# Order of loads on one DMA queue: column reloads behind the next weight chunks, and token tiles 14 and 15 loaded five stages later

## The chip, the cores and the metric

One core of a Trainium2 chip runs the whole kernel. The metric is the device time of one execution in microseconds (us). The time before is the median of three runs.

The core has a matrix engine (PE in the profile, with its weight loads as PEld), a vector engine (DVE), a scalar engine (ACT), a general engine (POOL) and a sync engine (SP). SP computes nothing: it issues transfers between the off-chip memory (HBM) and the on-chip memory in the order of the program. Sixteen DMA engines carry them out.

## The reference, cut to what matters

```python
x  = A_x                                   # 1 x 2048 x 512
xn = layernorm(x)
q, k, v = split(xn @ wqkv)                 # 32 heads of 16
pq, pk  = phi(q), phi(k)                   # phi(t) = (t+1 if t>0 else exp(t)) + 1e-6
kv = einsum("bhsd,bhse->bhde", pk, v);  z = sum_s pk
attn = (pq @ kv) / (pq . z + 1e-6) @ wo
h   = relu(xn @ w1 + b1) ** 2              # 512 -> 1376
out = x + attn + h @ w2 + b2
```

## The kernel before, in words

The 2048 tokens are cut into 16 tiles of 128 (NT = 16). Four tiles make a block (TB = 4), so there are four blocks. Numbers are float32, and most operands of products are held as a high and a low part, so that a product is three passes of the matrix engine over 128x512 operands.

**Stage 1, keys of every tile (loop over `i` at L801).** A tile is loaded by `load_x` (L157, transfer at L159), its mean and variance are measured on DVE (`measure`, L230), it is normalised into `xp`, and it must be transposed to become "columns" (features on the partitions). From tile 4 on this goes through HBM: `regroup` (L277) stores normalised tiles to a scratch tensor `via` (L281) and appends four reads to a list; `move` (L286) issues the listed reads at L289, into `xg` (into `xg4s` for tiles 4 and 5); DVE turns blocks of 32x32 (`turn`, L293) into a tile `t`, or `xT` for tiles 8 and up; ACT makes the high part `xs0h`/`xs1h` (L324) and DVE the low part `xs0l`/`xs1l` (L327). Then PE projects the columns of tile i onto the key weights (`project`, L369, 12 products into `pk`) and adds the outer products of the tile before it (`kx`, L389, 12 products). Tiles 4 and 5 are stored to `via` one by one, later tiles in pairs.

There are only two sets of columns, `xsb` (`xs0h`, `xs0l` and `xs1h`, `xs1l`), one block of four tiles each. So the columns of blocks 0 and 1 are stored to HBM, `xsd`, when blocks 2 and 3 are about to overwrite them: two stores of 1 MB at i = 4 and two at i = 7 (L811).

Raw tiles `x` alternate between two buffers of two tiles each (`two`, L91) beside two larger ones, so tiles 14 and 15 go where tiles 2 and 3 were.

**Stage 2, queries and the two-layer part, two passes (`for n in range(2)`, L941).** Pass 0 handles blocks 3 and 2, pass 1 blocks 1 and 0 (`t1`, `t2`). At the end of pass 0 a loop over `e` (L1285) adds the products of the second layer for one hidden chunk per step (`mlp_2`, 12 products on PE), while DVE, ACT and SP prepare pass 1. In that loop, in the order of the program:

```python
1289  if e:
1290      do(w2next, 2)                  # split the next piece of w2: high on ACT, low on DVE (L122)
...
1294  if e == 2:
1295      load_res(t2)                   # two 512 KB loads of x for the residual
...
1300  if n == 0 and 1 <= e < 5:          # reload of columns, 1 MB each
1302      nc.sync.dma_start(f32((x1, x2)[k][u]), xsd[(t1, t2)[k] - 2][u])
1303  do(prepare, ...)                   # sums of columns for pass 1, DVE and ACT (L671, L122)
1305  if e == 4:                         # last, narrow chunk of w1
1306      z = pair("w1z1"); zs = small_chunk(z)
1308  if e == 5: w = load_1("q", 0)      # two chunks of query weights, "rq"
1310  if e == 7: zs()                    # split of that chunk of w1, ACT then DVE (L119)
```

`small_chunk` loads by `raw_1` (three transfers at L184, named `r`, in runs of 256 and 128 bytes); the query weights are loaded at L714. These weights and the pieces of w2 (`r`, L165 and L207) rotate through six raw buffers, so each load waits for the last reader of the load six places before it. The narrow chunk of w1 takes the buffer of piece 4 of w2; the two query chunks take those of pieces 3 and 2. A wait on SP holds every transfer behind it. A transfer's semaphore, one of eight in turn, must also have been met by the transfer eight places before.

After the loop come the attention products of the four tiles (`add_attention`), the last two hidden chunks (`wait_for(last_two[...])`, which makes `s` from `r2c` on ACT and DVE, and for the narrow chunk copies a part of `s` by a transfer at L468), the sums to the output (L1054, stores at L1058), and pass 1 begins with `plain_1`, which reads the reloaded columns `xs0h`, `xs0l` and the narrow chunk; the columns `xs1h`, `xs1l` are first read a few products later. POOL adds the second bias to the residual by transfers of its own (L1046).

Of the kernel before, what the change touches and what calls it, by code (L numbers as in the profile page):

```python
# [18 lines left out]
def kernel(  # L19
# [58 lines left out]
    def bank(name, tag="ps"):  # L78
        return psum.tile([P, 512], F32, name=name, tag=tag)
# [6 lines left out]
    def next_tag(of):  # L86
        k, n = turns[of]
        turns[of][0] = (k + 1) % n
        return f"{of}{k}"

    def two(name):  # L91
        return keep.tile([P, 2, 512], F32, name=name, tag=next_tag("x"))
# [7 lines left out]
    def f32(ap):  # L100
        return ap.bitcast(F32)
# [55 lines left out]
    def load_x(i, t):  # L157
        n = t.shape[1]
        nc.sync.dma_start(t, xf[i * P:(i + n) * P, :].rearrange("(i p) d -> p i d", i=n))  # L159
        for k in range(n):  # L160
            xr[i + k] = t[:, k]
# [11 lines left out]
    def units(f):  # L173


        if f < NF - 1:
            return [(0, f * P, P)]
        return [(0, f * P + Q, 2 * Q), (2 * Q, f * P, Q), (3 * Q, f * P, Q)]

    def raw_1(f):  # L180
        t = w512(f"r1_{f}", "raw", 6)
        tj = t.rearrange("p (j n) -> p j n", j=NJ)
        for a, o, n in units(f):
            nc.sync.dma_start(tj[:, :, a:a + n], w1[:, o:o + n].rearrange("(j p) n -> p j n", j=NJ))  # L184
        return t
# [3 lines left out]
    def load_o():  # L189
        o = wos[0] = four("wo", "ra")  # L190
        for j in range(NJ):
            cut = P - Q * j
            for a, z, to in ((0, cut, Q * j), (cut, P, 0)):
                if z > a:
                    nc.sync.dma_start(o[to:to + z - a, j], wo[j * P + a:j * P + z, :])
# [52 lines left out]
    def normalise(tiles, st, mv, y):  # L248

        n = len(tiles)  # L250
        r, u = (y[:, k, :n] for k in range(2))
        if tiles[-1] >= NPE:

            nc.vector.scalar_tensor_tensor(u, mv[:, :n, 0], -1.0, r, op0=OP.mult, op1=OP.mult)
        later = []

        def last(i, o, src, k):
            nc.scalar.activation(o, src, AF.Identity, bias=u[:, k:k + 1], scale=r[:, k:k + 1])
            if i in groups:
                regroup(i)  # L260

        for k, i in enumerate(tiles):
            o, src = xp[i], xr[i]
            if i >= NDVE:

                o, src = o.rearrange("p g (j c) -> p g j c", j=NJ), gjc(src)
            if i < NPE:
                nc.vector.tensor_scalar(o, src, mv[:, k, 0:1], r[:, k:k + 1], op0=OP.subtract, op1=OP.mult)
                if i in groups:
                    regroup(i)  # L270
            else:
                later.append(lambda a=(i, o, src, k): last(*a))
        return later
# [12 lines left out]
    def move(n=8):  # L286
        for _ in range(n):
            if moves:
                nc.sync.dma_start(*moves.pop(0))  # L289
# [9 lines left out]
    def cols(i):  # L299

        return xsb[(i // TB + 1) % 2]
# [64 lines left out]
    def project(i, ps, w, steps, first=True, last=True):  # L366

        for n, (j, u, v) in enumerate(steps):
            nc.tensor.matmul(ps, lhsT=cols(i)[u][:, j, slot(i)], rhs=w[v][:, j, :], start=first and n == 0,  # L369
                             stop=last and n == len(steps) - 1)  # L370

    def parts(i):

        p = kp[i]
        pk[i] = pair(f"pk{i}")
        copy("act", pk[i][:, 0], p, 1e-6)
        nc.vector.scalar_tensor_tensor(pk[i][:, 1], p, 1e-6, f32(pk[i][:, 0]), op0=OP.add, op1=OP.subtract)
# [168 lines left out]
    for i0 in range(0, NT, TB):  # L546
# [5 lines left out]
        n = TB if i0 >= NPE else TB // 2  # L552
        if i0 < NPE:
            single = work.tile([P, 2, 512], F32, name=f"xg{i0}s", tag="r0")
            for k in range(2):
                i = i0 + k
# [3 lines left out]
        for k in range(0, n, 2):  # L560
            i = i0 + TB - n + k
            u, v = (t.rearrange("p a (g c) -> p (a g c)", g=NJ) for t in (a[:, TB - n + k:][:, :2], o[:, k:k + 2]))
            groups[i + 1] = [t.rearrange("p (g n) -> p g n", g=NJ) for t in (u, v)]
            u, v = (t.rearrange("p (g i c) -> p g i c", g=NJ, i=2) for t in (u, v))
# [89 lines left out]
    parts(0)  # L654
    phi_k(1, pks[1])
    normalise(*single)
    load_x(14, two("x14"))
    parts(1)
    tokens(1, "dve")
    measure(soon)  # L660
# [4 lines left out]
    def tokens_sum(n, tag):  # L665
        return keep.tile([P, 2, 2, 512], F32R, name=f"T{n}", tag=tag)
# [32 lines left out]
    def fetch():  # L699
        while todo and len(held) < 3:  # L700
            held.append(todo.pop(0)())
# [89 lines left out]
    def more(i=None):  # L791

        if i is None or i > 12:
            do(extra, counts[0].pop(0))
# [6 lines left out]
    for i in range(2, NT):  # L801
        if i == 13:
            nc.sync.dma_start(b1s[:, :NF - 1], b1[:(NF - 1) * P].rearrange("(f p) -> p f", p=P))
            for a, o, n in units(NF - 1):
                nc.sync.dma_start(b1s[a:a + n, NF - 1:], b1[o:o + n, None])
        move()
        if i in (4, 7):

            b = i // 7
            for u in range(2):  # L810
                nc.sync.dma_start(xsd[b][u], f32(cols(b * TB)[u]))  # L811
        if i == 9:
            load_o()
        if i > 10:
            fetch()
        ps = pks[i] if i < 3 else bank(f"pk{i}")
        if i > 2:
            project(i, ps, wk, HL)
        high = low = keep_t = lambda: None
        if i < NDVE:  # L820
            high, low, keep_t = transposed(i + 1)
        later = normalise(*soon) if i == 3 else []

        soon_turned = transposed(i + 2) if 11 <= i and i + 2 < NT else ()

        def mid():
            high()
            more(i)

        def late():  # L830
            low()
            more(i)

        if i == 12:
            rawz = raw_1(NF - 1)
            T.update({n: tokens_sum(n, f"B{n - 1}") for n in (1, 2)})
        if i == 12:
            w = load_1("q", 0)
        if i == 13:
            todo_1 = operands_first(0, w)  # L840
            extra.append(todo_1.pop(1))
        if i == 14:
            z = pair("w1z0")
            extra.append(lambda: split(z[:, 0], z[:, 1], rawz, "act", "dve"))
            o34 = halves(four("Tf", "r0"))
            extra.extend(sums_of(xT[NB - 1], xT[NB - 2], *o34))
            lows = [extra.pop() for k in range(2)]
            extra += [todo_1[0], lows[1], todo_1[1], lows[0], *todo_1[2:]]
        phi_k(i, ps, mid, late)
        more(i)  # L850
        run(*soon_turned)
        if i != 3:
            later = normalise(*soon) if soon else []
        parts(i)
        keep_t()
        if i == 2:
            tokens(2)
        if i + 1 < NT:
            tokens(i + 1)
        run(*later)  # L860
        if NDVE < i + 2 < 13:
            run(*transposed(i + 2))
        pieces(int(i > 11))
        if i == 2:
            ahead[3] = statistics(6, 7)
        if i + 2 in (4, 6, 8, 10):
            ahead[i + 2] = group(i + 6, i + 7)
        if i < 10:
            measure(ahead[(i + 2) // 2 * 2], i % 2)
        soon = ahead.get(i + 1, ())  # L870
        if soon:
            roots(*soon)
        kx(i - 1)
        more(i)
# [66 lines left out]
    for n in range(2):  # L941
# [128 lines left out]
        for p in range(NO + 1):  # L1070
            at_p = AT[p]
            kind, k = order[p] if p < NO else ("", 0)
            fa, fb = 2 * k, 2 * k + 1

            was, k = order[p - 1] if p else ("", 0)
# [209 lines left out]
        for e, f in enumerate(waiting[:-2]):  # L1285
            mlp_2(acc, f, s.pop(f))
            if e + 3 < NF - 2:
                wait_for(waiting[e + 3])
            if e:
                do(w2next, 2)  # L1290
                if e + 8 < NF:
                    g = waiting[e + 8]
                    w2next.extend(piece_2(g, place(g)))
            if e == 2:
                load_res(t2)
            if e == 4:
                bias = add_bias()
            if e in ((5, 6) if n else (7, 8)):
                do(bias)
            if n == 0 and 1 <= e < 5:  # L1300
                k, u = divmod(e - 1, 2)
                nc.sync.dma_start(f32((x1, x2)[k][u]), xsd[(t1, t2)[k] - 2][u])
            do(prepare, (1, 0, 0, 1, 0, 2, 2, 3, 1, 3, 1)[e])
            if n == 0:
                if e == 4:
                    z = pair("w1z1")
                    zs = small_chunk(z)
                if e == 5:
                    w = load_1("q", 0)
                if e == 7:  # L1310
                    zs()
            step(AE[e])
            if e and 0 < len(parts_2) and len(steps[t2]) <= 5 * (len(parts_2) - 1):
                do(parts_2)
# [55 lines left out]
```

## Time and profile before

| what | us |
|---|---|
| median of three runs | 410.63 |
| lowest and highest of them | 410.39, 410.93 |
| the profiled execution, its own time | 410.41 |
| its span, first to last instruction | 408.7 |
| PE busy | 403.8 |
| DVE busy | 304.7 |
| ACT busy | 262.2 |

The mean granted clock of PE was 0.999. The span is the part that the profile shows; 1.7 us of the profiled execution's time lie around it. In the rows below, the first number is a start in microseconds after the span's beginning and the second a duration; a name such as `xs1h<-xT` says which tile is written from which; `x4` counts merged instructions; a bracket at a row's end gives idle time of the engine just before and what ended it. SPq marks issues on the SP queue, whose duration is that of the issuing only. In rows on transfers the last number is the time from issue to landing. An end of a product on PE is modelled by the profiler, its start is not.

### The profile page before, as it was taken

The page shows a single profiled execution, that of the slowest core. Times are in us where ns is not written, and L with a number is a line of the kernel's source. Part 1 is how long each engine was busy: PE and PEld are TensorE (multiplying, and loading weights), DVE is VectorE, ACT ScalarE, POOL GpSimd, SP SyncE. Part 2 cuts the span into 40 slices and gives each one's busy share as a digit, 9 for nine tenths or more (in the row PEclk, how much of TensorE's full clock was granted, in tenths as well). Part 3 has the DMA queues.
Part 4 walks back from the last instruction along what each step waited for, and adds up shares of the span by engine and source line. Part 5 has one row for each costly group of instructions (what it writes and reads, how often), then busy time and mean ns, then how long its engine had stood idle before and what let it go on. Part 6 is the DMA issues. An engine that isn't in the chain of part 4 may idle for free.

```text
span 408.7 us, 5630 instructions
## 1 busy us (share of the span) xinstructions
PE 403.8 (99%) x1943; PEld 331.7 (81%) x1943; DVE 304.7 (75%) x556; ACT 262.2 (64%) x459; POOL 48.5 (12%) x81
## 2 busy tenths in 40 slices
PE   8999999999999999999999999999999999999996
PEld 7878888888788888888878887888888888878885
DVE  6886667487898989988349956567989586449833
ACT  4656777556888788886818641677587857837520
POOL 6343333220000000030000300000000200001200
PEclk9999999999999999999999999999999999999999
DMA  6969576810432231381557983321121881024612
GB/s 213 332 210 329 204 309 206 254 31 0 119 91 79 77 103 28 109 204 22 215 204 271 326 194 106 113 53 51 51 79 36 229 189 36 2 103 154 105 26 103
DMA packets 47182, 56.87 MB, mean 139 GB/s; under 512 B 8305, under 2 KB 30577, under 8 KB 45874
## 3 DMA queue, kind: packets, MB, share of 16 engines
q1 hardware_dynamic: 44850, 52.32, 39.3%
q0 software_dynamic: 2304, 4.20, 6.3%
q8 instruction: 15, 0.25, 0.2%
q14 instruction: 13, 0.11, 0.1%
HBM read 41.69 MB, written 13.63 MB: 135 GB/s over the span
## 4 chain that ended last, share of the span: by engine, by line
PE 85%; DMA 6%; DVE 5%; issue 1%; SPq 1%; ACT 1%; POOL 1%; DVEq 0%; ACTq 0%
PE b L488 33%; PE acc L130 29%; PE pk L369 9%; PE kx L389 9%; DMA r<-in_B_w_dram 4%; PE acc L499 2%; PE pz L130 1%; DVE s L119 1%; SPq L289 1%; PE b L130 1%; PE pz0b L130 1%; DMA x<-in_A_x_dram 1%; DMA via<-xp 1%; DMA xg4s<-via 1%; PE pt L308 0%
## 5 line engine op out<-in xcount | busy, mean ns | idle before, releaser
L130 PE MATMUL acc<-w2r,s 128*128 128x512 f32 x477 | 113.1, 390 | 0.4 <-DVE s L119 0.4
L130 PEld LDWEIGHTS acc<-w2r,s 128*128 128x128 f32 x477 | 89.4, 188 | 20.1 <-DVE s L119 0.8
L488 PE MATMUL b<-T,aop 128*128 128x512 f32 x336 | 83.4, 389 | 0.0
L488 PEld LDWEIGHTS b<-T,aop 128*128 128x128 f32 x336 | 63.0, 188 | 13.9 <-ACT t L111 0.8
L1046 POOL DMA_DIRECT2D res<-in_B_b_dram x16 | 14.4, 1091 | 277.2 <-DVE dt L430 87.4
L389 PE MATMUL kx<-pk,tok 128*128 128x512 f32 x192 | 46.3, 390 | 0.0
L389 PEld LDWEIGHTS kx<-pk,tok 128*128 128x128 f32 x192 | 35.9, 188 | 7.6
L488 PE MATMUL b<-xs0h,aop 128*128 128x512 f32 x112 | 36.9, 390 | 0.0
L130 PE MATMUL acc<-mh,aTsr 128*128 128x512 f32 x112 | 35.6, 389 | 0.0
L1054 DVE TENSOR_TENSOR res<-acc,res 128x512 f32<-128x512 f32 x16 | 11.0, 692 | 21.5 <-PE acc L130 19.2
L488 PEld LDWEIGHTS b<-xs0h,aop 128*128 128x128 f32 x112 | 21.0, 188 | 4.4
L130 PEld LDWEIGHTS acc<-mh,aTsr 128*128 128x128 f32 x112 | 21.0, 188 | 4.4
L119 POOL TENSOR_TENSOR tok<-xp,tok 128x512 fp32r<-128x512 f32 x15 | 19.8, 1322 | 38.9 <-ACT tok L111 38.9
L122 DVE TENSOR_TENSOR w2r<-r,w2r 128x512 fp32r<-128x512 f32 (+2 forms) x35 | 23.8, 681 | 0.5 <-ACT w2r L111 0.4
L111 ACT ACTIVATE aop<-S 128x512 fp32r<-128x512 f32 x28 | 17.5, 624 | 9.8 <-DVE S L728 9.8
L119 DVE TENSOR_TENSOR aop<-S,aop 128x512 fp32r<-128x512 f32 x28 | 19.3, 688 | 4.8 <-ACT aop L111 4.4
L119 DVE TENSOR_TENSOR s<-c,s 128x512 fp32r<-128x512 f32 x20 | 13.5, 689 | 11.4 <-ACT s L111 11.3
L488 PE MATMUL b<-xs0l,aop 128*128 128x512 f32 x56 | 21.8, 389 | 0.0
L130 PE MATMUL acc<-ml,aTsr 128*128 128x512 f32 x56 | 21.8, 389 | 0.0
L111 ACT ACTIVATE w2r<-r 128x512 fp32r<-128x512 f32 x32 | 19.6, 620 | 3.0 <-DMA out_dram<-res 2.0
L111 ACT ACTIVATE T<-Tf 128x512 fp32r<-128x512 f32 x16 | 9.5, 624 | 16.1 <-DVE Tf L671 16.0
L488 PE MATMUL b<-xs1h,aop 128*128 128x512 f32 x56 | 19.5, 389 | 0.0
(190 smaller groups left out, 742.9 us busy)
## 6 DMA issues: line engine op xcount, KB each, us to landing
r<-in_B_w_dram SPq DMA_DIRECT2D x49, 256.0 KB, 3.0
res<-in_A_x_dram SPq DMA_DIRECT2D x8, 512.0 KB, 4.2
res<-in_B_b_dram POOLq DMA_DIRECT2D x16, 256.0 KB, 5.8
out_dram<-res SPq DMA_DIRECT2D x15, 256.0 KB, 2.1
via<-xp SPq DMA_DIRECT2D x5, 512.0 KB, 3.2
xg<-via SPq DMA_DIRECT2D x20, 128.0 KB, 2.8
xTd<-t SPq DMA_DIRECT2D x8, 256.0 KB, 3.2
x<-in_A_x_dram SPq DMA_DIRECT2D x4, 512.0 KB, 6.4
```

Of the source, the lines that this page charges most:

```text
L111: nc.scalar.activation(o, i, AF.Copy, bias=bias)
L119: ENG[el].tensor_tensor(out=l, in0=src, in1=f32(h), op=OP.subtract)
L122: nc.vector.tensor_tensor(out=l, in0=src, in1=f32(h), op=OP.subtract)
L130: nc.tensor.matmul(ps, lhsT=a[u], rhs=b[v], start=first and n == 0, stop=last and n == 2)
L289: nc.sync.dma_start(*moves.pop(0))
L369: nc.tensor.matmul(ps, lhsT=cols(i)[u][:, j, slot(i)], rhs=w[v][:, j, :], start=first and n == 0, stop=last and n == len(steps) - 1)
L389: nc.tensor.matmul(kxp[c], lhsT=tok[i][:, u, c * P:(c + 1) * P], rhs=pk[i][:, v], start=i == 0 and (u, v) == first, stop=i == NT - 1 and ( ...
L488: nc.tensor.matmul(ps, lhsT=a[u][:, j * P:(j + 1) * P], rhs=b[v][:, j, :], start=first and j == 0 and n == 0, stop=last and j == 1 and n == 2,
L499: nc.tensor.matmul(ps, lhsT=s[u][:, k * P:(k + 1) * P], rhs=w2s[NF - 1][u][:, a:z], start=first and u == 0, stop=stop and u == 1)
L1046: nc.gpsimd.dma_start(r[:, i], b2[None, :].partition_broadcast(P), accum_op=OP.add)
L1054: nc.vector.tensor_tensor(out=r[:, a:z], in0=ps, in1=r[:, a:z], op=OP.add)
```

## The change

Two moves on the SP queue; PE, DVE, ACT and POOL keep their instructions and their order.

- The load of tiles 14 and 15 (512 KB) leaves the place behind the store of tile 4 to `via`. It now stands at i = 4, behind the reads of tiles 6 and 7 from `via` and ahead of the two 1 MB stores of columns to `xsd`.
- At the end of pass 0 the narrow chunk of w1 (three transfers) and the two chunks of query weights are issued one step earlier, and three of the four column reloads later: `xs0h` stays at e = 1, `xs0l`, `xs1h` and `xs1l` go from e = 2, 3, 4 to e = 5, 6, 7. The queue's order is now: `xs0h`, piece 10 of w2, the two residual loads, the narrow chunk, the two query chunks, `xs0l`, `xs1h`, the copy of a part of piece 10 (L211), `xs1l`.

```diff
@@ -654,7 +654,6 @@
     normalise(*single)
-    load_x(14, two("x14"))
     parts(1)
@@ -804,6 +803,8 @@
         move()
+        if i == 4:
+            load_x(14, two("x14"))
         if i in (4, 7):
@@ -1297,15 +1298,15 @@
-            if n == 0 and 1 <= e < 5:
-                k, u = divmod(e - 1, 2)
+            if n == 0 and e in (1, 5, 6, 7):
+                k, u = divmod((1, 5, 6, 7).index(e), 2)
                 nc.sync.dma_start(f32((x1, x2)[k][u]), xsd[(t1, t2)[k] - 2][u])
             do(prepare, (1, 0, 0, 1, 0, 2, 2, 3, 1, 3, 1)[e])
             if n == 0:
-                if e == 4:
+                if e == 3:
                     z = pair("w1z1")
                     zs = small_chunk(z)
-                if e == 5:
+                if e == 4:
                     w = load_1("q", 0)
```

## The prediction

> **What bounds the kernel now.** I read the page first: who is busy, and for how much of the span.
>
> ```profile
> span 408.7 us, 5630 instructions
> PE 403.8 (99%) x1943; PEld 331.7 (81%) x1943; DVE 304.7 (75%) x556; ACT 262.2 (64%) x459; POOL 48.5 (12%) x81
> ```
>
> PE is busy for 99%, and its instructions stay the same. A move of transfers can therefore only win the few places where PE stands still for an operand, and lose where it makes new ones. The second view is PE's waits, the third PE's timeline around them.
>
> ```profile
> PE acc L130 <- DVE s L119: 0.4, 1, 0.4
> ...
> PEld pk L369 <- ACT xs0h L324: 0.5, 1, 0.5
> ```
>
> ```profile
> 26.53 1.29 PE L389 MATMUL kx<-pk,tok 128*128 128x512 f32 x5
> 27.89 0.50 PE L369 MATMUL pk<-wkh,xs0h 128*128 128x512 f32 x1
> ...
> 33.63 2.72 PE pk L369 x12
> ...
> 49.84 0.39 PE L369 MATMUL pk<-wkh,xs1h 128*128 128x512 f32 x1
> ...
> 247.18 0.62 PE L130 MATMUL acc<-w2r,s 128*128 128x512 f32 x2
> 248.21 0.50 PE L130 MATMUL acc<-w2r,s 128*128 128x512 f32 x1 [0.41 <-DVE s L119]
> ```
>
> Twelve products take 2.72, so one starts every 0.227. The brackets use modelled ends, so I count by starts.
>
> - At 248: the two products from 247.18 start at 247.18 and 247.41, so the next was due at 247.64. It starts at 248.21, 0.57 late. It also lasts 0.50 instead of the 0.39 of an undisturbed one, 0.11 more. Price of the stop: 0.57 + 0.11 = **0.68**.
> - At 28: the fifth product from 26.53 starts at 27.44, so the next was due at 27.66 and starts at 27.89. Price: 0.23 + 0.11 = **0.34**.
>
> At 49.84 nothing is late today. That place matters below.
>
> **Part 1, the weights ahead of the reloads.** The chain of waits shows where the stop at 248 comes from; then the SP queue's issues, with two landings.
>
> ```profile
> 224.46 16.91 DMA r<-in_B_w_dram
> ...
> 241.48 0.64 ACT w1z L111
> ...
> 247.55 0.61 DVE s L119
> ```
>
> ```profile
> 221.77 0.47 SPq L1302 DMA_DIRECT2D xs0l<-xsd1l  x1
> ...
> 222.76 0.43 SPq L1302 DMA_DIRECT2D xs1l<-xsd0l  x1
> 223.29 10.97 SPq L184 DMA_DIRECT2D r<-in_B_w_dram  x3
> 234.37 4.51 SPq L714 DMA_DIRECT2D rq<-in_A_wqkv_dram  x2
> ```
>
> ```profile
> xs1l<-xsd0l SPq DMA_DIRECT2D x1, 1024.0 KB, 14.6
> ...
> s<-s SPq DMA_DIRECT2D x1, 128.0 KB, 2.2
> ```
>
> The narrow chunk of w1 is issued behind three reloads of 1 MB and lands at 224.46 + 16.91 = 241.37, behind the last of them (222.76 + 14.6 = 237.4). ACT splits it at once, and DVE's timeline shows what that held up.
>
> ```profile
> 223.99 0.68 DVE L122 TENSOR_TENSOR w2r<-r,w2r 128x512 fp32r<-128x512 f32 x1
> ...
> 228.35 0.69 DVE L122 TENSOR_TENSOR w2r<-r,w2r 128x512 fp32r<-128x512 f32 x1
> ...
> 236.25 1.42 DVE L671 TENSOR_TENSOR Tf<-xT,Tf 128x512 f32<-128x512 f32 x2
> 242.14 0.69 DVE L119 TENSOR_TENSOR w1z<-r,w1z 128x512 fp32r<-128x512 f32 x1 [4.47 <-ACT w1z L111]
> ```
>
> DVE is idle for 4.47 in front of that split, and `s`, for which PE waits at 248, stands further back in DVE's order. With the chunk issued where the reloads were, only the two residual loads are ahead of it. It should land some 10 us before 237.67, when DVE comes to it (236.25 + 1.42). Of the 4.47 there then remains about the ACT split of 0.64, so DVE runs 3.8 earlier and `s` is ready 3.8 - 0.57 = 3.2 before PE asks. The stop goes entirely: **-0.68**. Next in line is nothing of DVE's.
>
> What it costs: the second query chunk needs the buffer of piece 2 of w2, which DVE reads until 228.35 + 0.69 = 229.04 (the first query chunk, until 224.67). SP waits there, and behind it stand the three reloads, the copies at L211 and L468, and then the stores of results. The reloads so start at 229.0 instead of 221.8, 7.3 later, and the last would land near 237.4 + 7.3 = 244.7. The readers:
>
> ```profile
> 252.60 2.72 PE pz L130 x12
> ...
> 259.40 2.72 PE b L130 x12
> ```
>
> The first reads `xs0`, the second `xs1`; with the stop gone both come 0.68 sooner, which leaves about 14 us for the last reload. The cost here is nothing, covered by those products. The tightest is the copy at L468, which the narrow chunk's sums at about 248 need: it would have to be behind 244.7 by 3 us, and alone it takes 2.2.
>
> **Part 2, tiles 14 and 15 later.** Rows of the start on the SP queue, DVE, ACT, and the length of the moved load:
>
> ```profile
> 18.89 0.43 SPq L159 DMA_DIRECT2D x<-in_A_x_dram  x1
> ...
> 20.92 3.66 SPq L289 DMA_DIRECT2D xg4s<-via  x4
> ...
> 34.30 0.43 SPq L811 DMA_DIRECT2D xsd0h<-xs1h  x1
> ...
> 36.99 0.32 SPq L281 DMA_DIRECT2D via<-xp  x1
> ...
> 43.06 1.75 SPq L289 DMA_DIRECT2D xg<-via  x4
> ```
>
> ```profile
> 26.46 0.71 DVE L293 STREAM_TRANSPOSE t<-xg4s 128x512 f32<-128x512 f32 x1 [0.15 <-DMA xg4s<-via]
> ...
> 30.88 0.71 DVE L293 STREAM_TRANSPOSE t<-xg4s 128x512 f32<-128x512 f32 x1 [0.16 <-issue]
> ...
> 47.30 0.71 DVE L293 STREAM_TRANSPOSE xT<-xg 128x512 f32<-128x512 f32 x1 [0.37 <-DMA xg<-via]
> ```
>
> ```profile
> 27.21 0.63 ACT L324 ACTIVATE xs0h<-t 128x512 fp32r<-128x512 f32 x1 [1.47 <-DVE t L293]
> ...
> 48.05 0.63 ACT L324 ACTIVATE xs1h<-xT 128x512 fp32r<-128x512 f32 x1
> ```
>
> ```profile
> x<-in_A_x_dram SPq DMA_DIRECT2D x1, 512.0 KB, 6.0
> ...
> DMA packets 6807, 7.95 MB, mean 248 GB/s; under 512 B 482, under 2 KB 5602, under 8 KB 6547
> ...
> 36.00:43.00 7.00, 7.00 (x32) 5.78 (x31) 4.08 (x7) 4.10 (x8) 1.99 (x3) 1.00 0.99 396
> ```
>
> *The gain.* Tile 4's turn on DVE starts at 26.46, held 0.15 by the reads that follow the 512 KB load. Without the load they land earlier, and ACT (idle for 1.47) and PE follow: **-0.15**. Below: 0, since the next such turn shows the same 0.16 with nothing to wait for. Above: the whole 0.34. I take 0.15, the row of the wait itself.
>
> *The loss.* At i = 4 the load stands ahead of 2 MB of stores and of the store of tiles 8 and 9 to `via`, issued at 36.99, which must land before their reads can be issued at 43.06. From 36 to 43 the DMA engines are 99% busy at 396 GB/s, so what is put in front shifts the rest: 0.524 MB / 396 GB/s = 1.32. (The Trainium skill, "DMA: Bandwidth & Descriptors", section "Anatomy of one DMA — SWDGE (gpsimd) path", has a slope of 436 GB/s for another path, an estimate of 1.20; the sum below would be 0.12 lower by it. The measured rate decides.) DVE turns tile 8 at 47.30 after a wait of 0.37 for those reads, so it takes the shift in full. `xs1h` is ready at 48.05 + 0.63 = 48.68; ACT to PE takes 0.05 (27.21 + 0.63 = 27.84 against 27.89), so PE could start at 48.73 and does at 49.84. The slack is 1.11. The 0.15 of the start comes to DMA and PE alike. The stop is 1.32 - 1.11 + 0.11 = **+0.32**. Below: 0, when the shift is 1.1 or less. Above: 0.524 MB at the mean of 248 GB/s of the stretch from 18 to 50 is 2.11, a stop of 1.11. I take 396, the rate of the stretch itself. By tile 9 DVE should have made it up: no further stop.
>
> **Sum.** -0.68 - 0.15 + 0.32 = -0.51. The profiled execution took 410.41 (span 408.7 and 1.7 around it), which would become 409.9. It lies 0.22 below the median of 410.63, so for the median I forecast **410.1**. A difference of 0.2%, 0.82 here, is about what a measurement can tell from no change, so this is within it.
>
> **Rivals.**
>
> - *Tile 8 is not late.* The load is a read among stores; should they overlap, or should the turn of tile 5 and with it the queue come earlier, the 1.1 of slack holds. Then -0.68 - 0.15 to -0.68 - 0.34: 409.6 to 409.8, faster. Against it speaks the 99%, for it that only 0.2 is missing.
> - *Tile 8 is late by much more: slower.* The moved load took 6.0 to land where a copy with little ahead takes 2.2; if it holds the store of tiles 8 and 9 for those 3.8, PE stops for 3.8 - 1.11 + 0.11 = 2.8 and the sum is +2.0: 412.6. It decides from a shift of 1.8 on (a loss at all), beyond 0.2% from 2.7 on. Against it: the 396 GB/s.
> - *The copy at L468 lands late: slower.* Were nothing moved during SP's wait for the query chunk, the whole lot would land 7.3 later than the narrow chunk did, at 241.37 + 7.3 = 248.7, and the copy 2.2 after it, at 250.9. PE needs it just after 247.64, so it would stop for 3.3 + 0.11, and the sum is -0.68 + 3.41 + 0.17 = +2.9, 413.5. It decides from 3 us behind 244.7 on. Against it: until 229 the residual loads, the biases and the chunk keep the DMA engines at work. (The Trainium skill, same page, "Queues, rings and completion order", speaks for it: a transfer's semaphore lands only after all earlier writes of its DMA engine, so a small copy cannot overtake a reload. No run here shows it yet.)
> - *It does not do what it says at 248.* If another late operand stands behind `s`, part 1 brings nothing: -0.15 + 0.32 = +0.17, 410.8.
>
> **How the numbers follow.** Forecast 0.57, tile 8 not late 0.26, much later 0.08, the copy 0.04, no gain 0.05. Faster by over 0.2% is the first rival, 0.26; slower the second and third, 0.12; the rest 0.62. Low end: 409.6 and 0.1 for the runs' spread, 409.5. High end: the stop of 1.11 with no gain at the start, -0.68 + 1.11 = +0.43, 411.1. The slower rivals lie outside.
>
> **What would show it.** Right: no wait of PE for `s` near 247; the narrow chunk landed before 230; DVE's 4.47 under 1; the first product of tile 4 some 0.15 sooner; a new wait of PE for `xs1h` at 49.7, 0.2 to 0.4 long, behind reads issued 1.3 later. Wrong: no such wait, or one over 1; a wait near 247 for the copy or near 252 or 259 for columns.

## The result, and the profile after

| | before | after |
|---|---|---|
| median, us | 410.73 (6 runs, 410.07 to 411.07) | 415.08 (6 runs, 413.83 to 417.94) |
| ratio after to before | | 1.012 (1.0083 to 1.0157) |
| profiled execution, its span | 410.41, 408.7 | 417.94, 416.2 |

The changed kernel is slower by 1.2%, 4.4 us, where 0.5 us less was forecast in the sum and 410.1 for the median. Two of its runs, 417.94 and 417.10, have a mean granted clock of 0.995 instead of 1.000; the profiled execution is one of them, and the last section shows what that is. PE's waits in the profile after, with the sum in us, how often, and the longest:

```profile
PE pk L369 <- ACT xs1h L324: 3.4, 2, 3.3
PE b L488 <- ACT c L111: 1.6, 2, 1.3
```

The wait for `s` at 248 is gone, as forecast. The first line is the forecast wait for tile 8's columns, ten times as long. The second was not forecast at all: PE waits for a copy `c` that ACT makes near 268, at a place where the change moved nothing. The chain of waits shows both places, start and duration ahead of each step:

```profile
37.23 8.89 DMA via<-xp
47.45 4.66 DMA xg<-via
53.62 4.50 PE pk L369 x12
...
264.13 2.73 PE b L130 x12
...
266.95 0.63 ACT sz L111
267.58 0.48 ACT c L111
268.06 0.49 ACT t L111
```

The store of tiles 8 and 9 to `via` takes 8.89 to land, and the last of their reads 4.66. Then twelve products take 4.50 instead of 2.72: they are not only late but slow. Near 267 the chain goes from PE's products `b` at L130 to ACT's copy `sz` and from there to `c`. PE's timeline gives the length of the stop and the pace behind it:

```profile
47.48 2.88 PE L389 MATMUL kx<-pk,tok 128*128 128x512 f32 x12
53.62 0.80 PE L369 MATMUL pk<-wkh,xs1h 128*128 128x512 f32 x1 [3.26 <-ACT xs1h L324]
54.22 0.63 PE L369 MATMUL pk<-wkl,xs1h 128*128 128x512 f32 x1
54.64 0.63 PE L369 MATMUL pk<-wkh,xs1h 128*128 128x512 f32 x1
...
56.77 0.43 PE L369 MATMUL pk<-wkl,xs1h 128*128 128x512 f32 x1
57.04 1.09 PE L369 MATMUL pk<-wkh,xs1l 128*128 128x512 f32 x4
```

The twelfth product of the group at 47.48 starts at 49.98 by the trace, and the next at 53.62: 3.65 instead of 0.23, so 3.42 late. From 54.22 on the starts lie 0.427 apart instead of 0.227, until 56.77; with the first product's 0.37 this slowness costs 1.6. By PE's starts in this one execution the stop at tile 8 costs 3.42 + 1.6, the copies near 268 cost 2.45 (1.43, 0.53 and 0.19 at 266.5, 270.8 and 287.1, and 0.11, 0.11 and 0.08 for the product behind each), while 0.68 at 248 and 0.26 of the 0.34 at tile 4 are gained. That is 6.5 of the 7.5 by which the span grew. Of the rest 0.44 lies at the start, ahead of tile 4, where a second profile of the kernel before also differs from the first, by 0.26.

### The profile page after: what moved, and what is told of

Read it like the earlier page. It is cut to its first block, busy times and chain, and to the rows that moved or that the text cites. A ratio compares the mean times of both kernels' runs of the same rounds, so it can differ in the third digit from the quotient of the medians.

```text
span 416.2 us, 5627 instructions
## 1 busy us (share of the span) xinstructions
PE 406.7 (98%) x1943; PEld 332.2 (80%) x1943; DVE 304.0 (73%) x556; ACT 262.1 (63%) x459; POOL 47.7 (11%) x81
## 4 chain that ended last, share of the span: by engine, by line
PE 85%; DMA 5%; DVE 3%; ACT 3%; POOL 2%; SPq 1%; issue 1%; DVEq 0%; POOLq 0%; ACTq 0%
PE acc L130 37%; PE b L488 32%; PE kx L389 6%; PE pk L369 6%; DMA via<-xp 2%; PE acc L499 2%; PE pz L130 1%; DMA x<-in_A_x_dram 1%; DMA xg<-via 1%; PE b L130 1%; PE pz0b L130 1%; DVE k L364 1%; POOL y L246 1%; ACT pk L111 1%; DVE st L234 1%
## 5 line engine op out<-in xcount | busy, mean ns | idle before, releaser
L130 PE MATMUL acc<-w2r,s 128*128 128x512 f32 x477 | 112.8, 390 | 0.0
L130 PEld LDWEIGHTS acc<-w2r,s 128*128 128x128 f32 x477 | 89.4, 188 | 19.3 <-issue 0.7
L488 PE MATMUL b<-T,aop 128*128 128x512 f32 x336 | 84.0, 391 | 1.7 <-ACT c L111 1.6
L488 PEld LDWEIGHTS b<-T,aop 128*128 128x128 f32 x336 | 62.6, 188 | 17.0 <-ACT c L111 2.7
L488 PE MATMUL b<-xs0h,aop 128*128 128x512 f32 x112 | 36.9, 391 | 0.0
L130 PE MATMUL acc<-mh,aTsr 128*128 128x512 f32 x112 | 35.7, 389 | 0.0
L488 PEld LDWEIGHTS b<-xs0h,aop 128*128 128x128 f32 x112 | 21.0, 188 | 4.5
L130 PEld LDWEIGHTS acc<-mh,aTsr 128*128 128x128 f32 x112 | 21.0, 188 | 4.4
L488 PE MATMUL b<-xs0l,aop 128*128 128x512 f32 x56 | 21.8, 389 | 0.0
L130 PE MATMUL acc<-ml,aTsr 128*128 128x512 f32 x56 | 21.8, 389 | 0.0
L488 PE MATMUL b<-xs1h,aop 128*128 128x512 f32 x56 | 19.5, 389 | 0.0
```

The source lines that it names most:

```text
L130: nc.tensor.matmul(ps, lhsT=a[u], rhs=b[v], start=first and n == 0, stop=last and n == 2)
L488: nc.tensor.matmul(ps, lhsT=a[u][:, j * P:(j + 1) * P], rhs=b[v][:, j, :], start=first and j == 0 and n == 0, stop=last and j == 1 and n == 2,
```

## The experiments

Four kernels first took the change apart. Ratios are to runs of the kernel before on the same chip (its median there 410.9 to 411.1), with 95% intervals.

### Part 1 alone, and the buffer behind it

*Part 1 alone*: the diff without its two `load_x` lines.

> Part 1 alone (weights ahead of the reloads; tiles 14 and 15 loaded at the old place). Theory A, the rotation of the five pair buffers: the part of s for the narrow chunk of pass 1 (sz) falls on the buffer of the narrow chunk itself, so ACT waits for the last product that reads it and PE then for ACT; the stops of the changed kernel at 266 to 287, 1.54 + 0.64 + 0.27 = 2.45, stay, the stop of 0.68 at 248 is gone: 412.5. Rival B, the columns that are reloaded later: the same sum, but PE waits for columns or for the copy at L468. Rival C, the stops come only with the late tile 8 of part 2: then -0.68, 410.05.

Measured: 413.16, ratio 1.0053 (1.0035 to 1.0071). PE stops at 261.4, 265.7 and 282.0, for 1.43, 0.54 and 0.20, and nowhere else that the kernel before does not: about half of the loss lies in part 1. ACT's timeline of this kernel, and below it that of the kernel before at the same work:

```profile
261.87 0.63 ACT L111 ACTIVATE sz<-rz 128x512 fp32r<-128x512 f32 x1 [5.51 <-PE b L130]
262.40 0.58 ACT L111 ACTIVATE c<-b 128x512 f32<-128x512 f32 x1
262.88 0.59 ACT L111 ACTIVATE t<-b 128x512 f32<-128x512 f32 x1
```

```profile
262.16 0.69 ACT L476 ACTIVATE r2c<-b,b1s 128x512 f32<-128x512 f32 x1 [1.08 <-PE b L130]
262.75 0.93 ACT L111 ACTIVATE aop<-r 128x512 fp32r<-128x512 f32 x2
263.58 0.59 ACT L111 ACTIVATE c<-b 128x512 f32<-128x512 f32 x1
```

ACT stands idle for 5.51 in front of `sz<-rz`, the high part of the narrow hidden chunk of pass 1 (`hidden_last`), and what releases it is a product of PE, although `rz` is ACT's own work and long done. The reader is the buffer. `pair` (L97) hands out five buffers in turn. Moving `z = pair("w1z1")` from e = 4 to e = 3 moves it ahead of the pair of hidden chunk 2:

```
before:  2, z, 1, 10, 0, sz1     sz1 takes the buffer of hidden chunk 2, read before the loop's end
after:   z, 2, 1, 10, 0, sz1     sz1 takes the buffer of z, read by the products b<-xs1h,w1z (L130)
```

So the copy into `sz1` must wait for the last product that reads `w1z`, and behind it on ACT stand `c`, `t` and `T`, for which PE waits next. Two kernels test that. *The buffer alone*: the kernel before, with only the call of `pair` one step earlier; no transfer moves.

```diff
+                if e == 3:
+                    z = pair("w1z1")
                 if e == 4:
-                    z = pair("w1z1")
                     zs = small_chunk(z)
```

> The kernel before with one line moved: the pair buffer of the narrow chunk is taken at e = 3 and nothing else changes, no transfer moves. Theory A (rotation): the stops of 2.45 come, the one at 248 stays: about 413.1. Rival B (late reloads): 410.7, no change.

*Part 1 with the old turn*: the raw load is issued at e = 3 as in the change, and the pair buffer is taken at e = 4 (the lines below are its difference to part 1 alone).

```diff
-                if e == 3:
-                    z = pair("w1z1")
-                    zs = small_chunk(z)
+                if e == 3:
+                    rawz = raw_1(NF - 1)
                 if e == 4:
+                    z = pair("w1z1")
                     w = load_1("q", 0)
                 if e == 7:
-                    zs()
+                    split(z[:, 0], z[:, 1], rawz, "act", "dve")
```

> Part 1 with the raw load of the narrow chunk at e = 3 but its pair buffer taken at e = 4 as before; the order on every queue is that of part 1 alone. Theory A (rotation): ACT waits for no product at sz, the stops at 266 are gone and so is the one at 248: 410.73 - 0.68 = 410.05. Rival B (late reloads): 412.5 as with part 1.

Measured: the buffer alone 414.29, ratio 1.0073 (1.0053 to 1.0093); part 1 with the old turn 410.54, ratio 0.9984 (0.9971 to 0.9998). The same line of PE's waits stands in the profile of the buffer alone:

```profile
PE b L488 <- ACT c L111: 1.6, 2, 1.3
...
PE acc L130 <- DVE s L119: 0.5, 1, 0.5
```

It has the new stops (at 263.5, 267.8 and 284.1, for 1.42, 0.54 and 0.17) and keeps the old one for `s`; part 1 with the old turn has neither. So the turn of the buffer is the cause of the new stops, and the moved transfers themselves do what was forecast: a gain of 0.16%, 0.66 us, where 0.68 was the price of the stop. Of all the kernels that ran this one has the lowest ratio, with an interval that ends just below 1. The buffer alone came out 1.2 above its expectation of 413.1; its profile has one more stop, of 0.94 near 80, which is taken up below.

### Part 2 alone, and what a transfer costs at i = 4

*Part 2 alone*: only the two `load_x` lines of the diff.

> Part 2 alone (tiles 14 and 15 at i = 4, end of pass 0 as before). Theory A, the load in front of the stores makes tile 8 late by 3 us and more: PE stops for xs1h at about 50 for 2 to 4, in some runs followed by products at half pace; 413 to 415, and the time spreads over more than 1 us. Rival B, the loss of the changed kernel is all in part 1: then 410.4 to 410.9.

Measured: 412.63, ratio 1.0046 (1.0031 to 1.006), and stops in two places:

```profile
PE pk L369 <- ACT xs0h L324: 1.2, 1, 1.2
...
PE pk L369 <- ACT xs1h L324: 0.5, 1, 0.5
```

The second is tile 8's. The first is tile 6's, at 38.4 (1.40 late by starts): its reads were issued ahead of the moved load, and still their last one landed late. The next kernels vary what stands at that place.

*Half*: tile 14 at the old place, tile 15 (256 KB) at i = 4.

```diff
-    load_x(14, two("x14"))
+    t14 = two("x14")
+    load_x(14, t14[:, :1])
...
+        if i == 4:
+            load_x(15, t14[:, 1:])
```

> Of part 2 only half is done: tile 14 (256 KB) is loaded at its old place, tile 15 (256 KB) behind the moves of tiles 6 and 7; part 1 is left out. Part 2 whole gave 412.63 against 411.06, with PE stops of 1.4 for tile 6 and 0.63 for tile 8. Theory V (volume: what stands in the queue delays what follows by its bytes): both delays halve; the last reads of tiles 6 and 7 and the store of tiles 8 and 9 land half as late (1.5 instead of 3.1), the stop at tile 6 becomes 0.4 to 0.7 and the one at tile 8 goes, so the sum is +0.3 to +0.7, ratio 1.001 to 1.002. Rival R (place: a read queued behind the reads of tiles 6 and 7, whatever its size, holds up the last DMA engine): the stop at tile 6 stays at 1.2 or more, ratio 1.003 to 1.005.

*Wide*: rows of 4 KB, half as many. This kernel leaves out putting the two tokens of a row back into their order, so its output differs in tiles 14 and 15; the work and its order are the same otherwise.

```diff
+            t = two("x14")
+            nc.sync.dma_start(t, xf[14 * P:16 * P, :].rearrange("(p i) d -> p i d", i=2))
```

> Part 2 alone, but the moved load takes rows of 4 KB instead of 2 KB (each partition reads two neighbouring tokens, so the tokens of tiles 14 and 15 change places among themselves; same 512 KB). Theory V (volume): as part 2, stops of 1.2 to 1.5 for tile 6 and 0.4 to 3.4 for tile 8, ratio 1.0035 to 1.006. Rival D (single slow 2 KB reads of x, up to 1.4 us each in the trace of the changed kernel, are what holds the last DMA engines): with half as many reads the late engines come 1 us or more sooner, the tile 8 stop goes and that of tile 6 halves, ratio 1.001 to 1.002.

*An extra store* of 512 KB, and of 2 MB, with the load at its old place:

```diff
+        if i == 4:
+            spare = dram.tile([P, 2, BT], F32, name="spare")
+            nc.sync.dma_start(spare, f32(wk[0])[:, :2])      # 2 MB: wk[0] and wk[1] whole
```

> The kernel before with one more 512 KB store (the key weights, which nobody reads back) at the place where part 2 puts its load of 512 KB; the load itself stays at its old place. It tells what 512 KB cost there as a store from what they cost as a read of x. Theory B (bytes at the rate of the stretch): the store of tiles 8 and 9 lands 1.3 later, PE stops 0.3 for tile 8 and not at all for tile 6, ratio 1.000 to 1.0015. Rival K (any 512 KB there hold the store up by some 3, as the read did): it lands 2.5 to 3.1 later, stops of 1.4 at tile 6 or 0.6 to 2 at tile 8, ratio 1.003 to 1.005.

> The same with 2 MB of stores instead of 512 KB. Theory B: the store of tiles 8 and 9 lands 2.1 MB / 396 GB/s = 5.3 later, less the 1.1 of slack a PE stop of 4.2 to 4.4 for tile 8. It tells also whether the slow products after the long stop of the changed kernel belong to the stop: if a stop of more than 3 halves the pace of the next 8 products (0.427 instead of 0.227 each), 1.6 come on top, 5.9 in all, ratio 1.014; if not, 4.3, ratio 1.0105.

> The extra 512 KB store once more, for a second profile. In the first the store of tiles 8 and 9 was 1.1 late and the stop at tile 8 0.35, as bytes at 396 GB/s give, but the median was 1.004 all the same. If the rest is a later step of the chain that starts late (tile 14 near 80): a stop of 0.6 to 1.5 there, again with 0.3 to 0.5 at tile 8 and none at tile 6. If the loss was of that profile's chance: no stop at 80, ratio 1.000 to 1.002.

*An extra read* of 512 KB, of weights and of `x`, with the load at its old place:

```diff
+        if i == 4:
+            spare = four("spare", "ra")[:, :2]
+            nc.sync.dma_start(spare, wo[:2 * P, :].rearrange("(i p) d -> p i d", i=2))   # or xf[14 * P:16 * P, :]
```

> The kernel before with one more 512 KB read at the place of part 2's load: rows of 2 KB of the output projection's weights, into a buffer that is not in use yet; tiles 14 and 15 are loaded at their old place. Theory R (a read costs more there than a store of the same size): from 36 to 38 the DMA engines move under 280 GB/s instead of 406, the turn of tile 6 waits 3.0 or more for its reads instead of 1.46, the store of tiles 8 and 9 lands 2.6 to 4.0 later, ratio 1.004 to 1.006. Theory X (it is reading x there, beside the reads of via and the stores): as the 512 KB store, 400 GB/s or more, no wait beyond 1.5 at tile 6, the store 1.1 late.

> The same read of 512 KB, but of the rows of x that tiles 14 and 15 use, which have been read once already at the old place. By R and by X alike: under 280 GB/s from 36 to 38, a wait of 3.0 or more at tile 6, the store of tiles 8 and 9 2.6 to 4.0 late, ratio 1.004 to 1.006; if it comes out as the 512 KB store did (1.1 late), it was the load's absence from its old place that cost, not its presence at the new one.

*The kernel before, a second profile*:

> The kernel before once more, for a second profile: does the stop near 80 for tile 14, which eight of the other profiles show, come without any change? If it belongs to a chain that was shifted: none, as in the first profile, and the turn of tile 6 waits 1.4 to 1.5. If it is chance: 0.3 to 1.0.

What was measured, one line for each profile. "36 to 38" is the rate in the windows view; "turn of 6" is DVE's wait for the reads of tile 6; "reads of 8" is the start of the reads of tiles 8 and 9, which wait for the store to `via`; stops are by PE's starts.

| at i = 4 | GB/s, 36 to 38 | turn of 6 | reads of 8 | stop at 6, at 8 | ratio |
|---|---|---|---|---|---|
| nothing (before) | 406 | 1.46 | 43.06 | 0, 0 | |
| nothing (before again) | 425 | 1.32 | 43.11 | 0, 0 | |
| store 512 KB | 433 | 1.44 | 44.16 | 0, 0.35 | 1.0041 (1.0026 to 1.0055) |
| store 512 KB again | 379 | 1.53 | 44.89 | 0, 0.39 | 1.0037 (1.0023 to 1.0051) |
| store 2 MB | 423 | 1.39 | 48.46 | 0, 4.74 | 1.018 (1.0149 to 1.0211) |
| read 256 KB (half) | 360 | 1.46 | 44.00 | 0, 0.39 | 1.002 (1.0004 to 1.0035) |
| read 512 KB (part 2) | 188 | 3.09 | 46.07 | 1.40, 0.63 | 1.0046 (1.0031 to 1.006) |
| read 512 KB (after) | 252 | 1.69 | 46.14 | 0, 3.42 | 1.012 (1.0083 to 1.0157) |
| read 512 KB, wide | 277 | 3.25 | 45.72 | 1.58, 0.17 | 1.0053 (1.0037 to 1.0068) |
| extra read, weights | 241 | 1.39 | 46.46 | 0, 3.28 | 1.008 (1.006 to 1.01) |
| extra read, x | 92 | 3.58 | 46.80 | 1.83, 0.63 | 1.0096 (1.0059 to 1.0133) |

The rate is read here, in the windows view of the extra 512 KB store and of the extra read of x (DMA share and GB/s are the last two columns):

```profile
36.00:38.00 2.00, 2.00 (x10) 1.66 (x9) 0.71 (x1) 1.02 (x3) 0.92 (x2) 1.00 1.07 433
38.00:40.00 2.00, 2.00 (x10) 1.68 (x9) 1.40 (x4) 1.65 (x3) 0.00 (x0) 1.00 1.00 422
```

```profile
36.00:38.00 2.00, 2.00 (x11) 1.65 (x10) 0.00 (x0) 1.15 (x2) 1.14 (x2) 1.00 0.69 92
38.00:40.00 2.00, 1.28 (x6) 0.74 (x4) 0.48 (x1) 0.00 (x0) 0.00 (x0) 1.00 0.99 390
```

And the turns of tiles 6 and 8 on DVE's timeline, again of the extra store and of the extra read of x:

```profile
37.15 0.71 DVE L293 STREAM_TRANSPOSE t<-xg 128x512 f32<-128x512 f32 x1 [1.44 <-DMA xg<-via]
...
48.71 0.71 DVE L293 STREAM_TRANSPOSE xT<-xg 128x512 f32<-128x512 f32 x1 [1.85 <-DMA xg<-via]
```

```profile
39.52 0.71 DVE L293 STREAM_TRANSPOSE t<-xg 128x512 f32<-128x512 f32 x1 [3.58 <-DMA xg<-via]
...
51.23 0.71 DVE L293 STREAM_TRANSPOSE xT<-xg 128x512 f32<-128x512 f32 x1 [2.01 <-DMA xg<-via]
```

Three things follow for the place.

- Stores cost what the forecast's arithmetic says: 512 KB move the reads of tile 8 by 1.1 (1.8 the second time, of which the store's own later issue is 0.6), 2 MB by 5.4, which is 2.1 MB at 388 GB/s (the stop was 4.74, somewhat over the 4.2 to 4.4 expected, and slow products came behind it).
- A read of the same 512 KB costs 2.7 to 3.7, whether it reads `x` or weights, in rows of 2 KB or of 4 KB, and the rate between 36 and 38 falls to 92 to 277. So it is not the rows' size (the wide load failed to help) nor `x` as such.
- The shift is paid in one of two ways, and the profiles of one kernel differ in which: in three of the five profiles in the table with 512 KB of reads tile 6 is late by 1.4 to 1.8, PE so comes later to tile 8 and stops little there; in the other two (the changed kernel's first and the extra read of weights) tile 6 is in time and PE stops 3.3 to 3.4 at tile 8. The expectation that a read makes tile 6 wait 3.0 failed in the profile of the weights. Half the read stops PE for 0.39 at tile 8 and not at tile 6, while both of its expectations put the stop at tile 6.

What is not explained: the 512 KB store loses 0.4% in the median, 1.4 to 1.6 us, though its profiles show 0.5 at tile 8. Both also stop at 80 (0.59 and 0.31), where `xs0h` of tile 14 holds ACT up ahead of a copy that PE needs. But the second profile of the kernel before has that stop as well, 0.71 long, with nothing changed, and it took 411.20 where the first took 410.41:

```profile
PE kx L389 <- ACT pk L111: 0.6, 1, 0.6
```

The buffer alone, which moves no transfer, has it too, 0.94 long. By PE's starts seven of the sixteen other profiles show it, where the expectation says eight. So this stop belongs to the kernel before too, and how far an extra transfer makes it more frequent stays open. Nor is it fully explained why the extra reads lose 0.8 to 1% where part 2 alone loses 0.46%. Part 2 has 0.34 of gain at tile 4, which is not enough. Two of the six executions of each extra read, the longest ones (415.26 to 418.65), had a mean granted clock of 0.990 to 0.995, as after slow products; of the ten of part 2 none was below 0.999.

### The load elsewhere, and the parts together

*The load behind the moves of tiles 8 and 9* (`if i == 5:` instead of 4), without part 1; and *together with part 1 with the old turn*:

> The kernel before with the load of tiles 14 and 15 moved further back, behind the moves of tiles 8 and 9 (i == 5) instead of 6 and 7; part 1 left out. Theory V: nothing stands ahead of the reads of tiles 6 to 9 any more, so both stops go; the gain of 0.15 to 0.34 at tile 4 stays: ratio 0.999 to 1.000, unless the reads of tiles 10 and 11 take over the stop (then a stop for xs0h or xs1h of tile 10 of 0.5 to 1.5, ratio 1.001 to 1.004). Rival (the loss comes from taking the load out of its old place, not from the new place): the stops at tiles 6 and 8 stay, ratio 1.0035 or more.

> Part 1 with the buffer of w1z taken at its old turn (e == 4), and the load of tiles 14 and 15 behind the moves of tiles 8 and 9. If the two add up: 0.9984 for part 1 so mended times what the load at i == 5 gives (0.999 to 1.000), 0.9975 to 0.999, about 410.3 where the kernel before has 411.0; no PE stop near 248, 266 or for tiles 6 and 8. If the later load costs something at tiles 10 to 15: a stop there and a ratio over 1.000.

Measured: 411.81, ratio 1.0025 (1.0014 to 1.0035), and 411.10, ratio 1.0006 (0.9996 to 1.0015). No stop at tile 6 or 8 in either; both stop at 80, for 1.45 and 0.70, a place that neither expectation named. The load costs some 0.2% there too: 1.0006 against 0.9984 without it. That the stop at 80 is how it costs this is not shown, since the kernel before can have that stop as well. No later place that was tried is better than the old one.

*The changed kernel with the old turn of the buffer*, and *the changed kernel once more*:

> The changed kernel with only the turn of the buffer for w1z put back (raw load at e == 3, buffer taken at e == 4). If the two losses are the rotation of the buffers and part 2, and add up: part 1 so mended gave 0.9984 and part 2 alone 1.0046, together 1.003, about 412.3; no PE stop near 248, 264, 268 or 284, and the stops at tile 6 or 8 as in part 2 alone. If the reloads behind the query weights cost something beside the rotation: 1.006 or more.

> The changed kernel itself once more, for a second profile: its first showed a stop of 3.4 at tile 8 and none at tile 6, part 2 alone 1.2 at tile 6 and 0.5 at tile 8. If the order of the change decides, the first picture comes again (3 or more at tile 8, 1.6 of slow products behind it). If single late DMA engines decide, the stops of this profile differ from the first's, at tile 6, tile 8 or both, 1.2 to 3.4 together; the three stops behind 262 come again, 1.4, 0.5 and 0.2 long, in either case. Ratio 1.009 to 1.015.

Measured: 412.61, ratio 1.0046 (1.0025 to 1.0066), and 415.51, ratio 1.0115 (1.0094 to 1.0136). With the old turn PE has no stop at 248 nor behind 260; it stops 1.69 at tile 6 and 0.92 at tile 8. That is part 2's loss, some 2.5 to 3 us less than the whole change. The second profile of the change:

```profile
PE b L488 <- ACT c L111: 1.6, 2, 1.3
PE pk L369 <- ACT xs0h L324: 1.2, 1, 1.2
...
PE pk L369 <- ACT xs1h L324: 0.8, 2, 0.7
```

The line at L488 is the same to the tenth. The lines at L369 are part 2's other picture: 1.32 at tile 6 and 0.83 at tile 8, and no slow products. The two parts add up within their intervals: 1.0053 times 1.0046 of 411.06 is 415.1, and the change measured 415.08 and 415.51.

## Why the prediction was wrong, point by point

- **The stop at 248: right.** It is gone in every kernel with part 1, and its price, 0.68, came out as 0.66 (interval 0.1 to 1.2) where nothing else was changed. That the two agree so closely is luck: in the second profile of the kernel before the same stop costs 0.37 (PE starts 0.26 late at 249.0, and 0.11 follows), and in the wide load's profile, without part 1, it does not come at all. The DVE wait in front of `w1z` fell from 4.47 to 0.49:

```profile
243.63 0.69 DVE L119 TENSOR_TENSOR w1z<-r,w1z 128x512 fp32r<-128x512 f32 x1 [0.49 <-ACT w1z L111]
```

- **"The narrow chunk landed before 230": right, though not on the clock of the profile after.** There it was issued at 227.24 to 228.81 and landed near 232.5, but by then PE runs 5.4 behind the kernel before, because of tile 8 and the start. Part 1 alone, 0.4 behind, shows the place itself. The chunk's last transfer lands at 227.2:

```profile
222.16 1.58 SPq L184 DMA_DIRECT2D r<-in_B_w_dram  x3
225.08 4.73 SPq L714 DMA_DIRECT2D rq<-in_A_wqkv_dram  x2
229.87 0.59 SPq L1302 DMA_DIRECT2D xs0l<-xsd1l  x1
...
232.94 0.37 SPq L1302 DMA_DIRECT2D xs1l<-xsd0l  x1
239.06 0.48 SPq L468 DMA_DIRECT2D s<-s  x1
```

- **"The cost here is nothing, covered by those products": this step failed.** For the transfers it held: in part 1 alone the reloads went out from 229.9 on (forecast 229.0), the last landed at 246.1 (forecast 244.7), and neither columns nor the copy at L468 were waited for. But I followed only transfers, queues and the six raw buffers. The moved lines hold a call of `pair` too, and each such call takes a turn in five shared buffers. Its price was 2.45 by the stops, and 413.16 against 410.54, 2.6 us, in the medians. None of the rivals had it. The front of this document says that all engines keep their instructions and order; that is so, and the wait still changed, since a wait hangs on which buffer a tile gets.

- **The rival of the copy at L468: the mechanism is there, and it came close.** In part 1 alone the copy took 8.0 from its issue, not 2.2, with a reload of 1 MB ahead of it: it lands at 239.06 + 8.0 = 247.1, just behind the reload (246.1). PE's first product with the narrow chunk's `s` (L499) starts at 248.24, 1.2 later, so it did not wait. In the profile after the copy took 6.2 and 3.0 were left. The 2.2 were the row of a copy with little ahead of it.

```profile
xs1l<-xsd0l SPq DMA_DIRECT2D x1, 1024.0 KB, 13.1
s<-s SPq DMA_DIRECT2D x1, 128.0 KB, 8.0
```

```profile
248.24 0.62 PE L499 MATMUL acc<-w2r,s 128*128 128x512 f32 x2
```

  The Trainium skill, "DMA: Bandwidth & Descriptors", "Queues, rings and completion order", says that a semaphore's increment lands only after the earlier writes of its DMA engine; these rows agree.

- **The gain at tile 4: right.** In the profile after, DVE turns it at 26.65 without a wait and PE's stop of 0.34 shrinks to 0.08; 0.26 gained, more than the 0.15 forecast and within its bounds of 0 and 0.34. In all eight profiles in which the load or half of it is moved the stop there is 0.1 or less; with the whole load at its old place it is 0.2 to 0.6 in nine profiles and missing in one.

- **The loss at tile 8: right in place, mis-sized.** The step that failed is "I take 396, the rate of the stretch itself". 396 GB/s is what stores move there; the runs with extra stores confirm it for stores (388). The moved transfer is a read, and a read of 512 KB shifted the store by 2.7 to 3.7, which is 140 to 197 GB/s, below even the 248 that gave the upper end. The term of +0.32 became 3.42 + 1.6 at tile 8 in the profile after. The nearest row was quoted in the prediction and used for a rival only: the load's own 6.0 at its old place, which gave a shift of 3.8 and +2.0 in all. The changed kernel with the old turn of the buffer is what that sum describes: its ratio of 1.0046 is 1.9 us, and its stops add up to 2.8, as the rival said, but 1.8 of that at tile 6, where the rival had none. That rival had a chance of 0.08.

- **"No further stop": failed on both sides.** Tile 6 was not looked at, since its reads stand ahead of the load in the queue; being ahead did not protect their last packets. And behind the longest pauses PE itself is slow, so the stop's price is not only its length.

## What to carry to other kernels

When a step is moved in the program, list what each of its lines takes in turn: not only queues and transfers, but every allocation from a rotating pool, and for each later tile of that pool who read the buffer that it gets now. Price a moved transfer by its own row, in its own direction, not by the mean rate of the place where it goes. And where a chain of store, wait and read feeds PE, ask of the transfers ahead of the new one as well as of those behind it.

## What the runs showed of the hardware that was not expected

**A long pause of PE can be followed by slow products, and where it falls decides.** The granted clock (third column from the end) changes only at steps of 3.413 us in these profiles: the first stretch at full clock is 47.79 us (14 steps) in the three that slow down near 50, and 402.77 us (118 steps) in the kernel before. Here are such steps of the kernel with 2 MB of extra stores, where PE starts nothing from 50.11 to 55.08, of the extra read of weights, with a pause from 49.78 to 53.29, and of the extra read of x, with a pause from 38.89 to 40.95. The second number is the step's length, the third PE's busy time in it.

```profile
49.39:52.80 3.41, 1.10 (x5) 1.00 0.53 163
52.80:56.21 3.41, 1.14 (x3) 0.50 0.61 224
56.21:59.63 3.42, 3.42 (x10) 0.50 0.92 297
```

```profile
51.13:54.54 3.41, 1.25 (x5) 1.00 0.37 146
54.54:57.95 3.41, 3.41 (x9) 0.50 0.85 300
```

```profile
37.13:40.54 3.41, 2.15 (x10) 1.00 0.89 329
40.54:43.95 3.41, 3.00 (x13) 1.00 1.01 424
```

Steps in which PE was busy for 1.25 or less were followed by a step at half clock; so was the one of the changed kernel (0.36 busy from 50.00 to 53.41). Steps with 2.1 or more were followed by full clock in every profile here; nothing between was seen. That is why with the read of weights the slow pace began only 1.3 after PE had restarted. At half clock the starts lie 0.427 apart instead of 0.227: 2.2 were lost behind the pause of 4.97, 1.6 behind the changed kernel's of 3.65, and 1.7 behind that of 3.51. Behind the pauses of 0.86 to 2.06 (tiles 6 and 8) the pace was 0.227 at once. The Trainium skill, "TensorE: Matmul & The Clock Gate", "Part 1: The HAM clock gate", states an idle window of about 3.4 us after which the clock is halved, and 426.7 ns between products of 512 columns at half clock. The rows agree with the pace and with the window's length, but the window need not be idle throughout.

**A read of 512 KB queued among stores takes the place of two to three times its bytes at their rate** (2.7 to 3.7 us instead of 1.3), and in five of the seven profiles with such a read it held up reads that stand ahead of it. From 36 to 38 the DMA engines move 92 to 277 GB/s instead of 379 to 433, at a DMA share of 0.69 and more. The packets in the traces show a part of why: in the six profiles with rows of 2 KB, the typical one of the read's 256 packets takes 0.084 us, which over 16 engines is 390 GB/s, the rate of the stretch. But 12 to 40 of them take more than twice that, the longest 1.1 to 1.7 us. So reads are not slower throughout; single packets stand, nearly all of them before 38. Why they stand was not found.
